# The length-49 stage of a second Fourier transform: from split products on 98 rows to plain float32 products in the four quarters of TensorE

## The chip, the cores and the metric

The kernel runs on one core of one Trainium2 chip. The metric is the device time of one execution in microseconds (us). The engines are TensorE (PE; its weight loads are listed as PEld), VectorE (DVE), ScalarE (ACT), GpSimd (POOL) and SyncE (SP), whose queue starts nearly all DMAs. A change of over 0.3% either way is counted here as faster or slower.

## The reference

Three blocks follow one another on x of shape (2, 3136, 256); the change touches the transform of the third.

```python
def reference(**kwargs):
    x = attn_out                       # rfft over 3136, 256x256 complex mix, soft threshold, irfft
    x = _moe_ref(x=x, **moe_kwargs)    # layer norm, 256 -> 1024 -> 256 with relu, residual
    return _moe2_ref(x=x, **moe2_kwargs)

def _moe2_ref(x, w_ch1, w_ch2):
    X = np.fft.fft(x, axis=1)
    X = np.fft.fft(X, axis=2)
    mixed = np.real(X).astype(np.float32)
    u = x + mixed
    mu = np.mean(u, axis=-1, keepdims=True)
    var = np.mean((u - mu) ** 2, axis=-1, keepdims=True)
    un = (u - mu) / np.sqrt(var + 1e-06)
    ch = np.maximum(un @ w_ch1, 0.0) @ w_ch2
    return (u + ch).astype(np.float32)
```

## The kernel before

**Numbers.** Most matmuls take an operand in the type float32r, cut to a high and a low part (`h`, `l`), and add three products (`mm3r`: high by high, low by high, high by low; lines 228, 229 and 230). The three lines serve the first layers of both multilayer perceptrons (into the PSUM tiles `psa`) and several transform stages (into `psc`). Other matmuls are plain float32 products: the first transform's input stage (L331), part of its inverse (L368, L556) and the length-64 stages (L499, L511, L852).

**Order of the work.** After the first block come 13 chunks of the first perceptron (`mlp1`, 512, 384 or 256 rows each), then 13 chunks of the second (`mlp2`). `run_mlp` records for each chunk eight steps `l1` (a `psa` tile each, cut into `h` and `l` by ACT at L765 and DVE at L767) and up to four steps `l2` (L784 and L785 into `psb`, added to the residual by DVE). Between them it calls hooks at places such as (8, "l1", 6), which means chunk 8 behind step 6 of `l1`. A scheduler lays out each engine's order from that, and each engine works through its own in order.

**The stage that is changed.** A length of 3136 is 49 times 64. `Stage98` does the length-49 part of the second transform for each of the two batches: it reads the output of `mlp1` from DRAM (`dX1`, 98 rows of 8192; row 2n+s holds n of 49 and s of 2), multiplies by a 98 by 98 matrix, and writes `dA2` in DRAM. The matrix never mixes the two values of s, so half of it is zeros. Each `step` takes 512 of the 8192 columns, 16 steps per batch:

- `load` brings the columns in (L396), `split` cuts them into `h` and `l`. For batch 0 POOL does both parts (L408, L218). For batch 1 POOL first folds channel c with channel 256-c (L416 to L418, into a tile `w`), then ACT makes `h` (L210) and POOL makes `l` (L218).
- `mm3r` adds three products on 98 partitions into one `psc` tile (three `psc` tiles exist).
- The result is copied to a tile `o`: for batch 0 with the folding on ACT (L467) and DVE (L471, L472), for batch 1 by ACT (L210). Channel 128 comes from a small product made once per batch (`middle2`, L222 to L224). SP stores `o` (L476).

Batch 0 is done beside chunks 8 to 10 of `mlp1` (hooks `STAGE4_AT`), batch 1 beside chunks 1 to 3 of `mlp2` (`STAGE4_MLP2`). `Front` reads `dA2` back later (L836) and does the length-64 stage (L852, `stage_b`) and the channel transform (L877, `dmix`) through `psc` and `w` tiles, of which there are four (`WB`).

## Time and profile before

| | |
|---|---|
| time, median of 3 runs | 788.33 us (786.74 to 789.31) |
| profiled execution, own time | 788.44 us |
| its span, first to last instruction | 786.6 us |
| PE busy | 778.3 us (99%) |
| PEld busy | 662.7 us (84%) |
| DVE busy | 557.8 us (71%) |
| ACT busy | 374.4 us (48%) |
| POOL busy | 180.9 us (23%) |
| DMA, mean | 121 GB/s |

The profiled execution lies within the three runs, and 1.8 us of its time lie outside its span. Matmuls are pipelined: one matmul's row in a list gives the time until its result is there, which is longer than the distance to the next. The distances are read from the chain of work that ended last, where each piece is as long as it held up the end.

### The profile page before, as it was taken

The numbers are of one execution on the slowest core, as the hardware profiler recorded it, in microseconds if no ns is written. First come the engines' busy times: TensorE is split into PE (matmuls) and PEld (weight loads), VectorE is DVE, ScalarE is ACT, GpSimd is POOL, SyncE is SP. The second block draws the span as 40 slices with busy tenths as digits, with TensorE's granted clock in tenths as the row PEclk, the third lists the DMA queues.
The fourth block names the chain that finished last, engine by engine and source line by source line (L and its number), as shares of the span: only waits on it lengthen the run. The fifth ranks groups of instructions, "written<-read, shape, count | busy, mean of one in ns | idle before, by whom it ended". The sixth has DMA issues, their size and how long they took to land.

```text
span 786.6 us, 12135 instructions
## 1 busy us (share of the span) xinstructions
PE 778.3 (99%) x4306; PEld 662.7 (84%) x4306; DVE 557.8 (71%) x1253; ACT 374.4 (48%) x807; POOL 180.9 (23%) x198
## 2 busy tenths in 40 slices
PE   8999999999999999999999999999999999999997
PEld 3889987978888888988888998888888898888886
DVE  6799977687855889867875778546646657666643
ACT  0544356447954444555532346456643535444421
POOL 0464321263511111144420002466300000000000
PEclk9999999999999999999999999999999999999999
DMA  8951200630257233355743336554543334422211
GB/s 215 264 164 53 62 20 1 217 111 28 81 181 261 76 106 121 126 155 169 233 146 118 105 99 164 167 150 134 157 118 101 102 119 122 109 71 76 61 33 41
DMA packets 78911, 95.16 MB, mean 121 GB/s; under 512 B 17538, under 2 KB 59274, under 8 KB 78656
## 3 DMA queue, kind: packets, MB, share of 16 engines
q1 hardware_dynamic: 78772, 94.33, 39.9%
q8 instruction: 34, 0.56, 0.3%
q14 instruction: 25, 0.20, 0.1%
q10 hardware_dynamic: 80, 0.07, 0.0%
HBM read 56.89 MB, written 37.49 MB: 120 GB/s over the span
## 4 chain that ended last, share of the span: by engine, by line
PE 89%; DVE 4%; DMA 3%; issue 1%; SPq 1%; ACT 0%; POOL 0%; POOLq 0%; DVEq 0%
PE psb L784 23%; PE psb L785 12%; PE psa L228 12%; PE psa L230 11%; PE psa L229 11%; PE psb L532 5%; PE psc L852 3%; PE psc L228 2%; PE psc L230 2%; PE psc L229 2%; PE psc L368 2%; PE psa L499 2%; PE psc L877 1%; DMA q<-in_x_dram 1%; PE psc L553 1%
## 5 line engine op out<-in xcount | busy, mean ns | idle before, releaser
L765 ACT ACTIVATE h<-psa 128x512 fp32r<-128x512 f32 (+2 forms) x208 | 117.3, 572 | 198.8 <-PE psa L230 145.3
L767 DVE SCALAR_TENSOR_TENSOR h<-psa,h 128x512 fp32r<-128x512 f32 (+2 forms) x208 | 135.1, 654 | 61.9 <-ACT h L765 58.5
L784 PE MATMUL psb<-r3a,h 128*128 128x512 f32 x392 | 137.2, 395 | 0.0
L784 PE MATMUL psb<-r2b,h 128*128 128x512 f32 x392 | 136.8, 397 | 0.1
L785 PE MATMUL psb<-r3a,h 128*128 128x256 f32 x392 | 106.5, 281 | 0.0
L785 PE MATMUL psb<-r2b,h 128*128 128x256 f32 x392 | 105.9, 281 | 0.0
L532 PE MATMUL psb<-wm,h 128*128 128x256 f32 (+1 forms) x600 | 90.4, 297 | 0.1
L784 PEld LDWEIGHTS psb<-r2b,h 128*128 128x128 f32 x392 | 71.7, 188 | 15.9 <-issue 0.8
L784 PEld LDWEIGHTS psb<-r3a,h 128*128 128x128 f32 x392 | 71.9, 188 | 15.2
L532 PEld LDWEIGHTS psb<-wm,h 128*128 128x128 f32 (+1 forms) x600 | 78.1, 188 | 7.6 <-issue 5.5
L228 PE MATMUL psa<-u0r,r2b 128*128 128x512 f32 (+2 forms) x208 | 80.6, 388 | 0.0
L228 PE MATMUL psa<-u0r,r3a 128*128 128x512 f32 (+1 forms) x208 | 79.5, 382 | 0.0
L229 PE MATMUL psa<-u0r,r3a 128*128 128x512 f32 (+1 forms) x208 | 78.6, 378 | 0.0
L229 PE MATMUL psa<-u0r,r2b 128*128 128x512 f32 (+2 forms) x208 | 78.5, 378 | 0.0
L230 PE MATMUL psa<-u0r,r2b 128*128 128x512 f32 (+2 forms) x208 | 78.1, 380 | 0.0
L785 PEld LDWEIGHTS psb<-r3a,h 128*128 128x128 f32 x392 | 73.9, 189 | 3.9
L785 PEld LDWEIGHTS psb<-r2b,h 128*128 128x128 f32 x392 | 74.0, 189 | 3.3
L230 PE MATMUL psa<-u0r,r3a 128*128 128x512 f32 (+1 forms) x208 | 76.2, 378 | 0.0
L790 DVE TENSOR_TENSOR o<-psb,yb 128x256 f32<-128x256 f32 x74 | 30.3, 419 | 57.2 <-PE psb L785 55.9
L210 ACT ACTIVATE yg<-psc 98x512 f32<-98x512 f32 (+2 forms) x58 | 49.6, 866 | 37.7 <-PE psc L553 20.5
L218 POOL TENSOR_TENSOR u0r<-w,u0r 98x512 fp32r<-98x512 f32 (+2 forms) x28 | 37.3, 1346 | 95.5 <-ACT u0r L210 95.5
L218 POOL TENSOR_TENSOR h<-w 128x512 f32<-128x512 f32 (+1 forms) x26 | 34.7, 1335 | 84.5 <-DVE w L539 77.9
(141 smaller groups left out, 1368.2 us busy)
## 6 DMA issues: line engine op xcount, KB each, us to landing
dT<-q SPq DMA_DIRECT2D x19, 512.0 KB
q<-dT SPq DMA_DIRECT2D x19, 512.0 KB
s<-in_moe_w_ch_dram SPq DMA_DIRECT2D x16, 512.0 KB
dA<-o SPq DMA_DIRECT2D x32, 196.0 KB
dY<-yg SPq DMA_DIRECT2D x12, 512.0 KB
r<-dA SPq DMA_DIRECT2D x48, 128.0 KB
dX<-o SPq DMA_DIRECT2D x10, 512.0 KB
yb<-dX SPq DMA_DIRECT2D x50, 64.0 KB
```

The source lines that it names most:

```text
L210: nc.scalar.activation(out=o, in_=i, func=AF.Copy, scale=scale)
L218: ins = eng.tensor_tensor(out=o, in0=a, in1=b, op=ALU.subtract)
L228: nc.tensor.matmul(out=ps, lhsT=lh, rhs=rh, start=first, stop=False)
L229: nc.tensor.matmul(out=ps, lhsT=ll, rhs=rh, start=False, stop=False)
L230: ins = nc.tensor.matmul(out=ps, lhsT=lh, rhs=rl, start=False, stop=last)
L532: nc.tensor.matmul(out=ps[0:m, u * D:(u + 1) * D], lhsT=xv[:, o:o + m], rhs=wm_hl[wv][:, e, c, :], start=k == 0, stop=k == 11)
L765: ins = nc.scalar.activation(out=h[:, 0:n], in_=ps[:, 0:n], func=AF.Relu)
L767: ins = nc.vector.scalar_tensor_tensor(out=l[:, 0:n], in0=ps[:, 0:n], scalar=0.0, in1=h[:, 0:n], op0=ALU.max, op1=ALU.subtract)
L784: nc.tensor.matmul(out=ps, lhsT=h[:, ts_], rhs=w2[:, f, :], start=f == 0, stop=False)
L785: ins = nc.tensor.matmul(out=ps[:, 0:D], lhsT=l[:, ts_], rhs=w2[:, f, 0:D], start=False, stop=f == NF - 1)
L790: nc.vector.tensor_tensor(out=o, in0=ps[:, 0:D], in1=self.y[:, i, :], op=ALU.add)
L852: nc.tensor.matmul(out=ps, lhsT=self.raw[p][0:n, k, q * 128:(q + 1) * 128], rhs=self.cols(n, pr[k][1], im), start=True, stop=True)
```

## The change

Each step now takes 1024 columns, in two groups e of 512, so there are 8 steps per batch. The rows of s=0 lie on partitions 0 to 48 and those of s=1 on partitions 64 to 112. `quad` issues four plain float32 products per step: the product of s and e takes its 49 rows from the half s of the partitions, a 49 by 64 table from the same half, and writes 64 partitions in the half e of the PSUM tile of s. A step so fills two `psc` tiles. Splitting is gone; the folding of batch 1 stays and its result is the matmul's operand. The products for channel 128 take the same form with 16 columns. `dA2` is written by 64 stores of 49 rows where there were 32 of 98. The hooks go from 16 to 8 per batch.

```diff
@@ -14,7 +14,7 @@
 YB, HB, WB, SB = 4, 9, 4, 2
-R98, S98, O98 = 4, 8, 4
+R98, O98 = 4, 4
...
-STAGE4_AT = ((8, "l1", 6), (8, "l1", 7)) + tuple((8, "l2", i) for i in range(4)) + tuple(
-    (9, *at) for at in (("l1", 1), ("l1", 3), ("l1", 5), ("l2", 0), ("l2", 1), ("l2", 3))) + tuple(
-    (10, *at) for at in (("l1", 1), ("l1", 3), ("l1", 5), ("l2", 0)))
-STAGE4_MLP2 = tuple(
-    (1, *at) for at in (("l1", 1), ("l1", 3), ("l1", 5), ("l2", 0), ("l2", 1), ("l2", 2), ("l2", 3))) + tuple(
-    (2, *at) for at in (("l1", 1), ("l1", 3), ("l1", 5), ("l2", 0), ("l2", 1), ("l2", 3))) + tuple(
-    (3, *at) for at in (("l1", 1), ("l1", 3), ("l1", 5)))
+STAGE4_AT = ((8, "l1", 7), (8, "l2", 1), (8, "l2", 3), (9, "l1", 1), (9, "l1", 6), (9, "l2", 2), (10, "l1", 3), (10, "l2", 0))
+STAGE4_MLP2 = ((1, "l1", 3), (1, "l2", 0), (1, "l2", 2), (2, "l1", 1), (2, "l1", 5), (2, "l2", 1), (3, "l1", 1), (3, "l1", 5))
 STAGE4_FROM = ((7, "l2", 0), (0, "l1", 5))
...
@@ -107,7 +95,10 @@
     cs = ca.copy()
     for q in range(0, 96, 4):
         cs[:, q:q + 2], cs[:, q + 2:q + 4] = -ca[:, q + 2:q + 4], ca[:, q:q + 2]
-    t["ca"] = np.concatenate([ca, cs], 1)
+    cq = np.zeros((128, 128))
+    for s in range(2):
+        cq[64 * s:64 * s + N1, 0:N1], cq[64 * s:64 * s + N1, 64:64 + N1] = ca[s::2, s::2], cs[s::2, s::2]
+    t["ca"] = cq
     t["cam"] = cam.reshape(NQ, 128)
     t["cim"] = cim.reshape(128, NQ)
...
@@ -250,14 +239,13 @@
 
 
     ident = cp.tile([128, 128], F32, name="ident")
-    ca_hl = cp.tile([NQ, 2, 2 * NQ], F32R, name="ca_hl")
+    ca = cp.tile([128, 128], F32, name="ca")
     cam = cp.tile([NQ, 128], F32, tag="cam", name="cam")
     cam_hl = cp.tile([NQ, 2, 128], F32R, tag="cd", name="cam_hl")
     cim_hl = cp.tile([128, 2, NQ], F32R, name="cim_hl")
     cb = cp.tile([128, NK + 1, 128], F32, name="cb")
     cb0 = cp.tile([N2, 102], F32, name="cb0")
     ci0 = cp.tile([68, N2], F32, name="ci0")
-    ca_h, ca_l, cs_h, cs_l = (ca_hl[:, i % 2, i // 2 * NQ:(i // 2 + 1) * NQ] for i in range(4))
     g_sb = cp.tile([128, 2], F32, name="g_sb")
     e4 = cp.tile([128, 1], F32, name="e4")
 
...
@@ -373,70 +361,62 @@
             v = yg[self.b].rearrange("p j c -> p (j c)")
             sp.dma_start(out=dY[self.b][16 * c:min(16 * c + 16, NQ), :], in_=v[c:96:6, :] if c < 6 else v[96:98, :])
 
-    def s98():
-        return [next(s98_ring)[0:NQ] for _ in range(2)]
-
-
     class Stage98:
 
 
 
-        def __init__(self, src, dst, ch, cl, tag):
-            self.src, self.dst, self.ch, self.cl, self.tag = src, dst, ch, cl, tag
-            self.raw, self.hl = {}, {}
+        def __init__(self, src, dst, tag):
+            self.src, self.dst = (a.rearrange("(n s) f -> s n f", s=2) for a in (src, dst))
+            self.tag, self.raw, self.out = tag, {}, {}
             self.fold_last = src is dX1[0]
             self.g = self.nl = self.ns = 0
 
         def load(self):
             g = self.nl
-            if g >= 16:
+            if g >= 8:
                 return
-            n = 1 if self.fold_last else 2
-            t = wk.tile([NQ, 512], F32, tag="t98", name="r98", bufs=TB) if self.fold_last else stg()[0:NQ]
-            sp.dma_start(out=t, in_=self.src[:, g * 512:(g + n) * 512])
-            for e in range(n):
-                self.raw[g + e] = t[:, e * 512:(e + 1) * 512]
-            self.nl += n
-
-        def split(self):
+            t = next(s98_ring)
+            for s in range(2):
+                sp.dma_start(out=t[64 * s:64 * s + N1], in_=self.src[s][:, g * 1024:(g + 1) * 1024])
+            self.raw[g] = [t[:, e * 512:(e + 1) * 512] for e in range(2)]
+            self.nl += 1
+
+        def fold(self):
             g = self.ns
-            if g >= 16:
+            if g >= 8 or self.fold_last:
                 return
-            t = self.raw.pop(g)
-            if self.fold_last:
-                h, l = s98()
-                nc.gpsimd.tensor_copy(h, t)
-                sub(nc.gpsimd, l, t, h)
-                self.hl[g] = (h, l)
-                self.ns += 1
-                return
-            f = wslot(n=NQ)
-            v, w = (a.rearrange("q (j c) -> q j c", c=D) for a in (t, f))
-            lo, hi = v[:, :, 1:128], v[:, :, 255:128:-1]
-            nc.gpsimd.tensor_tensor(out=w[:, :, 1:128], in0=lo, in1=hi, op=ALU.add)
-            nc.gpsimd.tensor_tensor(out=w[:, :, 129:256], in0=lo, in1=hi, op=ALU.subtract)
-            nc.gpsimd.tensor_copy(w[:, :, 0:256:128], v[:, :, 0:256:128])
-            h, l = s98()
-            a_copy(h, f)
-            sub(nc.gpsimd, l, f, h)
-            self.hl[g] = (h, l)
+            for e in range(2):
+                f = wslot()
+                v, w = (a.rearrange("q (j c) -> q j c", c=D) for a in (self.raw[g][e], f))
+                lo, hi = v[:, :, 1:128], v[:, :, 255:128:-1]
+                nc.gpsimd.tensor_tensor(out=w[:, :, 1:128], in0=lo, in1=hi, op=ALU.add)
+                nc.gpsimd.tensor_tensor(out=w[:, :, 129:256], in0=lo, in1=hi, op=ALU.subtract)
+                nc.gpsimd.tensor_copy(w[:, :, 0:256:128], v[:, :, 0:256:128])
+                self.raw[g][e] = f
             self.ns += 1
 
+        def quad(self, c, v, n=512):
+
+            ps = [psum(self.tag) for _ in range(2)]
+            for e in range(2):
+                for s in range(2):
+                    ins = nc.tensor.matmul(out=ps[s][64 * e:64 * e + 64, 0:n], lhsT=ca[64 * s:64 * s + N1, c:c + 64],
+                                           rhs=v[e][64 * s:64 * s + N1], start=True, stop=True)
+            mark["pe"] = getattr(ins, "ins", ins)
+            return ps
+
         def middle(self):
 
-            t = wk.tile([NQ, 32], F32, tag="m98", name="m98", bufs=1)
-            hl = wk.tile([NQ, 2, 32], F32R, tag="mhl", name="mhl", bufs=1)
-            sp.dma_start(out=t, in_=self.src.rearrange("q (j c) -> q j c", c=D)[:, :, 128])
-            self.mid_in = t, hl
+            t = wk.tile([128, 32], F32, tag="m98", name="m98", bufs=1)
+            for s in range(2):
+                sp.dma_start(out=t[64 * s:64 * s + N1], in_=self.src[s].rearrange("n (j c) -> n j c", c=D)[:, :, 128])
+            self.mid_in = t.rearrange("q (g e j) -> q e g j", e=2, j=2)
 
         def middle2(self):
-            t, hl = self.mid_in
-            nc.gpsimd.tensor_copy(hl[:, 0], t)
-            sub(nc.gpsimd, hl[:, 1], t, hl[:, 0])
-            ps = psum(self.tag)
-            mm3(ps[0:NQ, 0:32], cs_h, cs_l, hl[:, 0], hl[:, 1], True, True)
-            self.mid = wk.tile([NQ, 32], F32, tag="mid", name="mid", bufs=1)
-            a_copy(self.mid, ps[0:NQ, 0:32])
+            ps = self.quad(64, [self.mid_in[:, e] for e in range(2)], 16)
+            self.mid = wk.tile([128, 2, 16], F32, tag="mid", name="mid", bufs=1)
+            for s in range(2):
+                a_copy(self.mid[:, s], ps[s][:, 0:16])
 
         def start(self):
             self.middle()
@@ -444,36 +424,35 @@
             self.load()
 
         def ahead(self):
-            self.split()
-            if self.fold_last:
-                self.load()
-            self.split()
+            self.load()
+            self.fold()
 
         def step(self):
             g = self.g
-            if g >= 16:
+            if g >= 8:
                 return
             if g == 0:
                 self.middle2()
-            if self.nl <= g + (3 if self.fold_last else 4):
+            if self.nl <= g + 3:
                 self.load()
-            self.split()
-            h, l = self.hl.pop(g)
-            ps = psum(self.tag)
-            mm3r(ps[0:NQ, :], self.ch, self.cl, h, l, True, True)
-            o = wk.tile([NQ, 512], F32, tag="r98", name="o98", bufs=R98) if self.fold_last and g % 2 else next(o98_ring)[0:NQ]
-            if self.fold_last:
-                v, w = (a.rearrange("q (j c) -> q j c", c=D) for a in (ps[0:NQ, :], o))
-                ins = nc.scalar.activation(out=w[:, :, 0:128], in_=v[:, :, 0:128], func=AF.Copy)
-                with tc.issue_after(getattr(ins, "ins", ins)):
-                    a_copy(w[:, :, 128], self.mid[:, 2 * g:2 * g + 2])
-                lo, hi = w[:, :, 1:128], v[:, :, 255:128:-1]
-                nc.vector.tensor_tensor(out=w[:, :, 129:256], in0=lo, in1=hi, op=ALU.subtract)
-                nc.vector.tensor_tensor(out=lo, in0=lo, in1=hi, op=ALU.add)
-            else:
-                a_copy(o, ps[0:NQ, :])
-                nc.gpsimd.tensor_copy(o[:, 128:512:256], self.mid[:, 2 * g:2 * g + 2])
-            sp.dma_start(out=self.dst[:, g * 512:(g + 1) * 512], in_=o)
+            self.fold()
+            ps = self.quad(0, self.raw.pop(g))
+            for s in range(2):
+                o = wk.tile([128, 512], F32, tag="r98", name="o98", bufs=R98) if self.fold_last and s else next(o98_ring)
+                mid = self.mid[:, s, 2 * g:2 * g + 2]
+                if self.fold_last:
+                    v, w = (a.rearrange("q (j c) -> q j c", c=D) for a in (ps[s], o))
+                    ins = nc.scalar.activation(out=w[:, :, 0:128], in_=v[:, :, 0:128], func=AF.Copy)
+                    with tc.issue_after(getattr(ins, "ins", ins)):
+                        a_copy(w[:, :, 128], mid)
+                    lo, hi = w[:, :, 1:128], v[:, :, 255:128:-1]
+                    nc.vector.tensor_tensor(out=w[:, :, 129:256], in0=lo, in1=hi, op=ALU.subtract)
+                    nc.vector.tensor_tensor(out=lo, in0=lo, in1=hi, op=ALU.add)
+                else:
+                    a_copy(o, ps[s])
+                    nc.gpsimd.tensor_copy(o[:, 128:512:256], mid)
+                for e in range(2):
+                    sp.dma_start(out=self.dst[s][:, (2 * g + e) * 512:(2 * g + e + 1) * 512], in_=o[64 * e:64 * e + N1])
             self.g += 1
 
 
@@ -966,9 +945,7 @@
     todo = {}
 
     def l_ca():
-        t = stg()[0:NQ, 0:4 * NQ]
-        sp.dma_start(out=t, in_=t_ca.rearrange("q h c -> q (h c)"))
-        a_copy(flat(ca_hl), t)
+        sp.dma_start(out=ca, in_=t_ca)
         halves(cim_hl, tab["cim"])
 
     def l_cim():
...
@@ -1155,9 +1132,9 @@
 
     for ch in mlp1[1:12] + mlp2[1:]:
         ch.by_act = True
-    s98_ring = ring(u0[:, 0:4096], S98, 512)
+    s98_ring = ring(u0[:, 0:4096].bitcast(F32), 4, 1024)
     o98_ring = ring(cp.tile([128, O98 * 512], F32, tag="wm", name="o98"), O98, 512)
-    s4 = [Stage98(dX1[b], dA2[b], ca_h, ca_l, "c") for b in range(NB)]
+    s4 = [Stage98(dX1[b], dA2[b], "c") for b in range(NB)]
     hooks = {}
 
     def after(k, i, f):
```

PE, behind a step of the second layer in chunk 8 of `mlp1`; before (`ca_hl` is the split table, `psc` the stage's PSUM tile):

```order
L784 MATMUL psb<-r3a,h 128x512
L785 MATMUL psb<-r3a,h 128x256
L228 MATMUL psc<-u0r,ca_hl 98x512
L229 MATMUL psc<-u0r,ca_hl 98x512
L230 MATMUL psc<-u0r,ca_hl 98x512
L228 MATMUL psa<-u0r,r3a 128x512
```

The same place now (line numbers are those of the changed file, in which L228 to L230 are L217 to L219 and L784 and L785 are L763 and L764; `x4` stands for four rows in a line):

```order
L763 MATMUL psb<-r3a,h 128x512
L764 MATMUL psb<-r3a,h 128x256
L403 MATMUL psc<-u0r,ca 64x512 x4
L217 MATMUL psa<-u0r,r3a 128x512
L218 MATMUL psa<-u0r,r3a 128x512
```

Four float32 products stand together where three float32r products stood, for twice the columns. 14 of the 16 steps stand so. The other two, both of batch 0, stand in two pieces; PE in chunk 9, before:

```order
L785 MATMUL psb<-r3a,h 128x256
L228 MATMUL psc<-u0r,ca_hl 98x512
L229 MATMUL psc<-u0r,ca_hl 98x512
L230 MATMUL psc<-u0r,ca_hl 98x512
L228 MATMUL psc<-u0r,ca_hl 98x512
L229 MATMUL psc<-u0r,ca_hl 98x512
L230 MATMUL psc<-u0r,ca_hl 98x512
L230 MATMUL psa<-u0r,r3a 128x512
```

And now:

```order
L219 MATMUL psa<-u0r,r3a 128x512
L403 MATMUL psc<-u0r,ca 64x512 x2
L217 MATMUL psa<-u0r,r3a 128x512
L218 MATMUL psa<-u0r,r3a 128x512
L219 MATMUL psa<-u0r,r3a 128x512
L217 MATMUL psa<-u0r,r3a 128x512
L218 MATMUL psa<-u0r,r3a 128x512
L219 MATMUL psa<-u0r,r3a 128x512
L403 MATMUL psc<-u0r,ca 64x512 x2
L217 MATMUL psa<-u0r,r3a 128x512
```

The two products of group 0 and the two of group 1 are apart, with six products of the first layer between them. With the products for channel 128, PE goes to quarters and back 19 times: 10 times in batch 0 and 9 times in batch 1.

## Rows read from the trace of the kernel before

**Rows 1.** The page, part 1 (busy us, share, instructions) and part 2 (slices).

```profile
PE 778.3 (99%) x4306; PEld 662.7 (84%) x4306; DVE 557.8 (71%) x1253; ACT 374.4 (48%) x807; POOL 180.9 (23%) x198
...
PE   8999999999999999999999999999999999999997
```

**Rows 2.** The page, part 4: the chain that ended last, by engine.

```profile
PE 89%; DVE 4%; DMA 3%; issue 1%; SPq 1%; ACT 0%; POOL 0%; POOLq 0%; DVEq 0%
```

**Rows 3.** Windows: a plain chunk, batch 0's stretch, batch 1's stretch.

```profile
core 0: us, PE busy (x) PEld busy (x) DVE busy (x) ACT busy (x) POOL busy (x), PEclk, DMA share, GB/s
...
258.20:280.40 22.20, 22.20 (x114) 18.81 (x113) 20.24 (x45) 10.56 (x23) 3.28 (x2) 1.00 0.36 120
354.50:420.00 65.50, 65.50 (x325) 53.93 (x324) 48.16 (x116) 31.70 (x85) 23.22 (x24) 1.00 0.54 170
490.00:569.00 79.00, 78.86 (x418) 65.68 (x417) 45.99 (x117) 44.41 (x98) 44.82 (x74) 1.00 0.52 153
```

**Rows 4.** The stage's split table `ca_hl`: durations in ns (min/median/max), forms.

```profile
L228 PE MATMUL psc<-u0r,ca_hl x32: 391/394/479, 354.9 to 566.4; 98*98 98x512 f32 x32
L229 PE MATMUL psc<-u0r,ca_hl x32: 389/396/398, 355.2 to 566.7; 98*98 98x512 f32 x32
L230 PE MATMUL psc<-u0r,ca_hl x32: 389/397/472, 355.5 to 566.9; 98*98 98x512 f32 x32
```

**Rows 5.** Chain, 354.0 to 358.5 us: start, us held, what.

```profile
354.91 0.02 PE psc L222
354.93 0.09 PE psc L223
355.01 0.09 PE psc L224
...
357.25 0.23 PE psc L228
357.48 0.23 PE psc L229
357.71 0.23 PE psc L230
```

**Rows 6.** Chain, 103.0 to 104.8 us: a float32 product of 512 columns.

```profile
103.24 0.86 PE psc L368 x2
```

**Rows 7.** Timeline of PEld, 4.9 to 9.5 us: start, us, count, idle before.

```profile
5.39 0.19 PEld L331 LDWEIGHTS psa<-h,cam 98*128 98x128 f32 x1 [0.24 <-issue]
5.82 0.19 PEld L331 LDWEIGHTS psa<-h,cam 98*128 98x128 f32 x1 [0.24 <-issue]
6.25 0.19 PEld L331 LDWEIGHTS psa<-h,cam 98*128 98x128 f32 x1 [0.24 <-issue]
```

**Rows 8.** Line 556: float32 with 64 columns of weights.

```profile
L556 PE MATMUL psc<-h,ci x4: 379/404/430, 97.9 to 167.2; 68*64 68x256 f32 x4
```

**Rows 9.** Chain, 595.5 to 597.5 us: products on 64 rows, then 128.

```profile
596.27 0.58 PE psc L852 x4
596.85 0.42 PE psc L877 x2
```

**Rows 10.** Chain, 428.5 to 435 us: the same lines, all on 128 rows.

```profile
432.69 0.45 PE psc L877 x4
433.14 0.84 PE psc L852 x8
```

**Rows 11.** Line 218, 480 to 570 us: batch 1's low parts on POOL.

```profile
L218 POOL TENSOR_TENSOR u0r<-w,u0r x16: 1282/1293/1303, 489.6 to 558.6; 98x512 fp32r<-98x512 f32 x16
```

**Rows 12.** Line 408: batch 0's high parts on POOL.

```profile
L408 POOL CAST u0r<-r x16: 612/614/1080, 341.9 to 402.0; 98x512 fp32r<-98x512 f32 x16
```

**Rows 13.** Line 210, 480 to 570 us: batch 1's high parts and copies on ACT.

```profile
L210 ACT ACTIVATE u0r<-w x16: 613/629/638, 488.9 to 557.9; 98x512 fp32r<-98x512 f32 x16
L210 ACT ACTIVATE o<-psc x16: 577/597/609, 497.9 to 567.4; 98x512 f32<-98x512 f32 x16
```

**Rows 14.** Line 476: the stores of the stage on SP's queue.

```profile
L476 SPq DMA_DIRECT2D dA<-o x32: 307/322/2547, 357.4 to 568.3; - x32
```

**Rows 15.** Line 416: the first of batch 1's two folding operations.

```profile
L416 POOL TENSOR_TENSOR w<-stg x16: 725/732/912, 485.6 to 555.9; 98x254 f32<-98x254 f32 x16
```

More of the change, by code (lines that the diff above doesn't have):

```diff
@@ L69 @@
 NF = DFF // 128
-def _round12(v):
-    b = v.astype(np.float32).view(np.uint32).astype(np.uint64)
-    b += 0x7FF + (b >> 12 & 1)
-    return (b & 0xFFFFF000).astype(np.uint32).view(np.float32)
 def _tables():
@@ L161, in _tables @@
     out = {"ident": ident.astype(np.float32)}
-    for k in ("cam", "cim", "cb", "ci", "cb0", "ci0", "cd"):
+    for k in ("ca", "cam", "cim", "cb", "ci", "cb0", "ci0", "cd"):
         out[k] = t.pop(k).astype(np.float32)
-    for k, v in t.items():
-        h = _round12(v)
-        out[k] = np.ascontiguousarray(np.stack([h, _round12(v - h)], 1))
+    assert not t
     return out
```

## The prediction

> **What bounds the kernel now.** I read the page's busy times first: PE is busy 99% of the span and every slice between the first and the last is at 90% or more [rows 1]. The chain that ended last says the same: 89% of it is PE [rows 2]. Then the two stretches that the change touches, by windows. Beside batch 0 PE is busy all of 65.5 us, beside batch 1 78.86 of 79.0 us, at granted clock 1.00, while POOL, ACT and DVE have room: POOL 23.2 and 44.8 us, ACT 31.7 and 44.4 us [rows 3]. So a microsecond of PE's order in these stretches is a microsecond of the end, and work taken from POOL or ACT is worth nothing by itself. The reader should carry one number into the sum: how long PE is held, per 1024 columns, by the old and by the new form.
>
> **What is removed from PE.** The stage has 32 groups of three products [rows 4]. Their rows give 0.39 us each, but that is the time to the result; in the chain each holds PE 0.23 us [rows 5], in some places 0.24, so a group holds it 0.70 us and 1024 columns hold it 1.40 us. The three small products for channel 128 hold it 0.20 us (0.02, 0.09 and 0.09) [rows 5]. Removed: 32 x 0.70 + 2 x 0.20 = 22.8 us.
>
> **What one float32 product costs.** A plain float32 product of 512 columns stands in the trace as two matmuls, and both together hold the chain for 0.86 us [rows 6], 0.43 us each. Rows and weight columns do not enter: L331, on 98 rows with 128 columns of weights, goes at the same distance of 0.43 us [rows 7]. So the four products of a step are eight halves of 0.43 us, 3.44 us if nothing runs side by side and 0.86 us if all four quarters do. The old form took 1.40 us. Everything depends on where between these two it falls.
>
> **How the halves overlap.** No two matmuls of the old kernel use different parts of the array at once, so this must be bounded. What the trace does show is the order. In a row of float32 products the weights of each half are loaded 0.43 us after those of the half ahead (5.39, 5.82, 6.25 us) [rows 7], the distance of the matmuls themselves: here loads run one matmul ahead and not two. The halves of a product follow each other in the program and use the same quarter. So the second half of the first product must wait 0.43 us for its own quarter, and the first half of the second product stands behind it. It can then run beside that second half, from which it differs in rows, but not beside the first. I take this staircase as the likeliest: a product starts when the second half of the product ahead has started and its own weights are in. Those take 0.05 us for 64 columns: the float32 matmul with 64 weight columns lasts 430 ns where it waited for its load and 379 where it did not [rows 8]. Four products then take 3 x (0.43 + 0.05) + 0.86 = 2.30 us, two of them 0.48 + 0.86 = 1.34 us.
>
> **What going to quarters and back costs.** Line 852 has a few products on 64 rows, which are the nearest rows. Four of its matmuls behind full-size ones hold the chain 0.58 us, and the two of L877 behind them 0.42 [rows 9]; on 128 rows eight of L852 hold it 0.84, so four 0.42, and four of L877 0.45, so two 0.22 [rows 10]. Going there costs 0.16 us and coming back 0.20, together 0.36 us. For the low bound I keep nothing, in case quarters of 64 columns do not need it; I take 0.36, since these rows change the rows used as the new form does. The Trainium skill's page TensorEngine Tiling (Array Packing), section Key Properties, says that changing the tiling mode drains TensorE; the rows just named agree, with 0.36 us a round trip, and by the page's other statement, that a change of tile alone does not drain, there is nothing to add within a burst.
>
> **The sum on PE.** 14 steps stand as one burst: 14 x (2.30 + 0.36) = 37.2 us. Two steps stand in two pieces: 4 x (1.34 + 0.36) = 6.8 us. The products for channel 128 are eight short halves per batch, 0.05 us each by the weight load or 0.09 us by the old small products [rows 5]: 0.4 to 0.7 us, I take 0.5, together 1.0 us. One pair of them stands alone, one more round trip: 0.36 us. Added: 45.4 us. Less 22.8 us this is +22.6 us. The profiled execution took 788.44 us, 0.1 above the median, so the forecast is 811 us.
>
> **What else moves, and why it is set at nothing.** POOL loses 16 low parts of 1.29 us in batch 1 [rows 11] and 16 high parts of 0.61 us with their low parts in batch 0 [rows 12]; ACT loses 16 high parts of 0.63 us [rows 13]. None of it stands in the chain beside a PE that is always busy. The copies out of PSUM stay at two per 1024 columns and at 512 columns each; 0.60 us on ACT [rows 13]. SP gets 32 more stores, 8 more loads in batch 1 and two more small ones, 42 x 0.32 us [rows 14] = 13.4 us in some 130 us; the transposed inputs of later chunks go through the same queue and could land about 1 us later each. PE has no wait for them in these stretches today [rows 3], and a slower PE asks later. If that cover fell short in each of five chunks it would be about 5 us. Folding for batch 1 now writes into `w` tiles that are held until the burst. Two of the four are so taken, and `dmix` has to wait in three places until a burst has read its tile; DVE, which works in order, then holds back the next `l` part (L767). PE has three `psa` tiles of six products, 3 x 6 x 0.23 = 4.1 us, as cover against a burst of 2.66 us. Folding itself takes 2 x 2 x 0.73 us and two short copies per step [rows 15], where a step comes every 79/8 = 9.9 us, so PE should not wait for it. I take nothing, and up to 5 us for the range. With no cost for switching and no 0.05 us the likeliest case falls to 802 us; its own range is 802 to 816.
>
> **Rivals.**
> 1. *All four quarters at once.* If the second half of a product does not hold up the next product, a burst is 0.86 + 3 x 0.05 = 1.01 us and a piece 0.91. With switching: 14 x 1.37 + 4 x 1.27 + 1.36 = 25.6 us, +2.8 us, 791 us. Against it speaks the one-ahead order of the loads [rows 7]; for it, that nothing in the trace shows a matmul held up by another quarter. The Trainium skill, page TensorE: Matmul & The Clock Gate, section Part 3: Packing small matmuls, says that matmuls in different tiles start about 4 ns apart and run together; by that figure a burst is 0.87 us before switching, an estimate that gives about 789 us. The same section says that matmuls start and end in program order, which makes the staircase for products of two halves. No run shows yet which of the two holds here.
> 2. *All four at once, and no cost for switching*: 14 x 1.01 + 4 x 0.91 + 1.0 = 18.8 us, -4.0 us, 784 us. This is the case on the other side. It decides once a burst with all that surrounds it holds PE less than some 1.2 us. Against it stand the 0.58 and 0.42 us around line 852 [rows 9].
> 3. *Two streams*, one for each half of the rows, each in its own order: three halves one behind the other, 1.29 + 0.05 = 1.34 us. 14 x 1.70 + 4 x 1.27 + 1.36 = 30.2 us, +7.4 us, 796 us.
> 4. *No overlap at all*, the change does not do what it says: 3.44 us a burst and 1.72 a piece, 14 x 3.80 + 4 x 2.08 + 1.36 = 62.9 us, +40 us, 828 us. For it speaks that no row shows an overlap of matmuls at all.
>
> **Chances.** Staircase 0.47, no overlap 0.12, two streams 0.11, all at once with switching 0.12, all at once without 0.18. The range leaves out the case at 828 us and reaches to the others: 783 to 816 us. Faster by over 0.3% is the last case, 0.18. Within 0.3% is half of the fourth, 0.06. Slower is the rest, 0.76.
>
> **What the profile of the changed kernel would show.** For the staircase: in a burst of L403 the weight loads of the eight halves start about 0.05 and 0.43 us apart in turn, and the burst holds PE about 2.3 us. If all start within 0.2 us it is rival 1 or 2; if each is 0.43 us behind the last it is rival 4. For switching: 0.16 us of pause ahead of the first load of L403 and 0.20 behind the last. PE should still be busy near 99%; POOL should fall by some 50 us and ACT by some 10 us, with no gain in time. Idle on PE inside chunks 1 to 3 of `mlp2`, released by POOL's folding or by DVE, would mean that the `w` tiles are the new wait. I would be wrong above all if quarters are served out of the program's order, or if plain float32 in a quarter costs other than 0.43 us a half.

## The result and the profile after

| | before | after |
|---|---|---|
| time, median of 5 runs each on one chip | 788.33 us (786.74 to 789.46) | 794.15 us (793.66 to 797.29) |
| ratio, 95% interval | | 1.0086 (1.0059 to 1.0113) |
| profiled execution: own time, span | 788.44, 786.6 us | 795.9, 794.1 us |

The change made the kernel slower, by 5.8 us where 22.6 were forecast. The page of the changed kernel, parts 1, 2 and 4, answers to [rows 1, 2]:

```profile
PE 782.5 (99%) x4348; PEld 652.9 (82%) x4348; DVE 550.6 (69%) x1253; ACT 365.0 (46%) x792; POOL 127.5 (16%) x146
...
PE   9999999999999999999999999998999999999997
...
PE 80%; DMA 9%; DVE 6%; issue 2%; SPq 1%; ACT 1%; POOL 1%; POOLq 0%; DVEq 0%; ACTq 0%
```

POOL lost 53 us and ACT 9 us, as foreseen, and nothing came of it. The chain is where the reader should stop: PE's share of it fell from 89% to 80%, and DMA's rose from 3% to 9%. Transfers now end last in places where PE did. Busy shares do not show this: PE is still at 99%.

**The burst.** A burst is the four products of one step in a row. The timeline of PE, a window of 0.2 us from 363.90, and the same burst in a longer window (start, us, count):

```profile
363.97 0.66 PE L403 MATMUL psc<-u0r,ca 49*64 49x512 f32 x4
363.97 1.09 PE L403 MATMUL psc<-u0r,ca 49*64 49x512 f32 x8
```

Two windows on line 403 inside the burst (us, PE busy with the number of matmuls, PEld the same, granted clock, DMA share, GB/s):

```profile
364.05:364.44 0.39, 0.39 (x4) 0.12 (x8) 1.00 0.18 63
364.44:364.48 0.04, 0.04 (x8) 0.00 (x0) 1.00 0.25 102
```

The timeline of PEld from 363.9 to 364.0 us, and the group of these loads by line 403 (ns min/median/max, first and last start in us):

```profile
363.96 0.15 PEld L403 LDWEIGHTS psc<-u0r,ca 49*64 49x64 f32 x4 [0.25 <-issue]
```

```profile
L403 PEld LDWEIGHTS psc<-u0r,ca x64: 129/132/135, 355.9 to 416.9; 49*64 49x64 f32 x64
L403 PE MATMUL psc<-u0r,ca x64: 589/604/640, 356.0 to 417.3; 49*64 49x512 f32 x64
```

One half lasts up to 0.640 us until its result is there, and four of them together last 0.66 us. Four loads take 0.15 us where one takes 0.13, so they start some 7 ns apart. These are the first halves of all four products. Until 364.44 us nothing else runs; the four second halves follow together from 364.45 us, 0.48 us behind the first. All four quarters run side by side from the start, and there is no staircase.

What a burst costs is read from the chain, for a piece of two products (four halves) and for a whole burst:

```profile
361.31 1.01 PE psc L403 x4
362.31 0.32 PE psb L764
...
363.92 0.12 PE psb L764
364.04 1.02 PE psc L403 x8
365.06 0.43 PE psa L217
365.48 0.23 PE psa L218
```

A burst holds PE 1.02 us, and the matmul behind it 0.43 in place of 0.23: 1.22 us, where the old form held it 1.40. A piece of two is as dear, 1.01 + (0.32 - 0.12) = 1.21 us, for half the columns. The products for channel 128 add 0.1 us to the piece that they stand in (1.13 us in the chain at 355.89). In batch 1 one pair of them stands alone, at 502.04 us. The chain runs over transfers there, so the price is read from a kernel of the experiments (stores on POOL's queue, loads held back), where the same pair stands at 499.86 us:

```profile
499.93 0.22 PE psc L403 x4
500.15 0.43 PE psa L217
```

Alone it holds PE 0.22 + (0.43 - 0.23) = 0.42 us, and the other pair adds 0.1 us to its burst. So PE's own order is 14 x 1.22 + 4 x 1.21 + 0.1 + 0.5 = 22.5 us against the 22.8 removed. By that the kernel should have come out even (-0.3 us).

**The waits.** PE's waits between 420 and 610 us in the changed kernel (what waited for whom, us in all, times, longest); before, PE was busy 78.86 of 79.0 us in batch 1's stretch [rows 3]:

```profile
PE psb L763 <- DVE mv L644: 1.8, 1, 1.8
PE psa L217 <- ACT u0r L199: 1.5, 1, 1.5
PE psa L217 <- DVE h L746: 0.5, 1, 0.5
PE psc L831 <- DMA r<-dA: 0.4, 1, 0.4
```

The timeline of PE at the first of them, and two windows behind the two long ones (us, PE busy, PEld, DVE, ACT, POOL, granted clock, DMA share, GB/s):

```profile
521.34 0.47 PE L763 MATMUL psb<-r2b,h 128*128 128x512 f32 x1 [1.77 <-DVE mv L644]
...
522.11 0.40 PE L763 MATMUL psb<-r2b,h 128*128 128x512 f32 x1
...
522.48 0.63 PE L763 MATMUL psb<-r2b,h 128*128 128x512 f32 x1
```

```profile
522.50:525.80 3.30, 3.30 (x12) 2.48 (x10) 1.54 (x5) 3.30 (x9) 2.26 (x7) 0.50 0.27 64
553.20:556.50 3.30, 3.30 (x8) 2.59 (x9) 2.13 (x9) 3.30 (x9) 0.00 (x0) 0.50 0.20 65
```

Behind each long wait stands a stretch at the lower clock level, 1.2 GHz (0.50), in which the same matmul takes 0.63 us and not 0.40. Each such stretch of at least 3.3 us does half its work, some 1.7 us lost. The waits at 519.57, 537.64 and 550.85 us and the two stretches make 1.77 + 0.51 + 1.48 + 2 x 1.7 = 7.2 us. With the 0.4 us for `r<-dA` and PE's order that is 7.3 us; the two profiled executions lie 7.5 us apart.

What is late at the two long waits is the transposed input of the next chunk (`dT<-q`, then `q<-dT` through SP; ACT and DVE cut it into parts, L199 and L207). SP's queue, ACT and DVE in the changed kernel, and behind them SP's two rows in the kernel before:

```profile
480.65 2.55 SPq L412 DMA_DIRECT2D m<-dX  x1
483.25 9.62 SPq L380 DMA_DIRECT2D u0r<-dX  x10
492.96 1.09 SPq L635 DMA_DIRECT2D yb<-dX  x2
494.15 1.85 SPq L779 DMA_DIRECT2D out_dram<-o  x3
496.05 0.54 SPq L635 DMA_DIRECT2D yb<-dX  x1
496.80 1.84 SPq L690 DMA_DIRECT2D dT<-q  x1
...
506.49 0.75 SPq L698 DMA_DIRECT2D q<-dT  x1
```

```profile
515.79 1.15 ACT L199 ACTIVATE u0r<-q 128x512 fp32r<-128x512 f32 x2 [5.82 <-DMA q<-dT]
516.46 1.29 DVE L207 TENSOR_TENSOR u0r<-q,u0r 128x512 fp32r<-128x512 f32 x2 [5.76 <-ACT u0r L199]
```

```profile
493.07 0.57 SPq L711 DMA_DIRECT2D dT<-q  x1
503.63 0.38 SPq L719 DMA_DIRECT2D q<-dT  x1
```

The ninth and tenth load of the stage (the fifth group) have no free place until POOL has folded the first group, so SP waits, and `dT<-q` behind them goes out 3.7 us later than before. DVE is done with its part at 517.75 us and only then comes to what stands behind it in its order, the additions that empty `psb` among it (L769 and L770, from 520.06 us); for these PE waits at 519.57 us. The short wait at 537.64 us has another origin: ACT could not copy into `o` until a store of the stage, `dA<-o` of 527.99 us, had landed at 536.18 us, and the cut of a `psa` tile that PE needed free stood behind that copy, on ACT and then on DVE.

### The profile page after: what moved, and what is told of

It is laid out like the page before. It is cut to its first block, busy times and chain, and to the rows that moved or that the text cites. A ratio compares the mean times of both kernels' runs of the same rounds, so it can differ in the third digit from the quotient of the medians.

```text
span 794.1 us, 12190 instructions
## 1 busy us (share of the span) xinstructions
PE 782.5 (99%) x4348; PEld 652.9 (82%) x4348; DVE 550.6 (69%) x1253; ACT 365.0 (46%) x792; POOL 127.5 (16%) x146
## 4 chain that ended last, share of the span: by engine, by line
PE 80%; DMA 9%; DVE 6%; issue 2%; SPq 1%; ACT 1%; POOL 1%; POOLq 0%; DVEq 0%; ACTq 0%
PE psb L763 21%; PE psa L217 11%; PE psb L764 11%; PE psa L219 10%; PE psa L218 10%; PE psb L511 5%; PE psc L831 2%; DMA q<-dT 2%; DMA dA<-o 2%; PE psc L356 2%; PE psa L478 2%; PE psc L403 2%; DMA q<-in_x_dram 1%; PE psc L856 1%; PE psc L532 1%
## 5 line engine op out<-in xcount | busy, mean ns | idle before, releaser
L763 PE MATMUL psb<-r2b,h 128*128 128x512 f32 x392 | 138.5, 400 | 1.8 <-DVE mv L644 1.8
L763 PE MATMUL psb<-r3a,h 128*128 128x512 f32 x392 | 137.3, 396 | 0.0
L764 PE MATMUL psb<-r2b,h 128*128 128x256 f32 x392 | 106.9, 282 | 0.0
L764 PE MATMUL psb<-r3a,h 128*128 128x256 f32 x392 | 106.1, 281 | 0.0
L763 PEld LDWEIGHTS psb<-r2b,h 128*128 128x128 f32 x392 | 72.5, 189 | 19.0 <-issue 3.8
L763 PEld LDWEIGHTS psb<-r3a,h 128*128 128x128 f32 x392 | 71.8, 188 | 16.3 <-ACT h L744 0.8
L217 PE MATMUL psa<-u0r,r2b 128*128 128x512 f32 (+2 forms) x208 | 82.4, 396 | 2.0 <-ACT u0r L199 1.5
L217 PE MATMUL psa<-u0r,r3a 128*128 128x512 f32 (+1 forms) x208 | 80.0, 384 | 0.1
L219 PE MATMUL psa<-u0r,r2b 128*128 128x512 f32 (+2 forms) x208 | 79.5, 386 | 0.0
L218 PE MATMUL psa<-u0r,r2b 128*128 128x512 f32 (+2 forms) x208 | 79.2, 381 | 0.0
L764 PEld LDWEIGHTS psb<-r3a,h 128*128 128x128 f32 x392 | 73.9, 189 | 5.5 <-issue 1.6
L764 PEld LDWEIGHTS psb<-r2b,h 128*128 128x128 f32 x392 | 74.7, 190 | 2.9
L219 PE MATMUL psa<-u0r,r3a 128*128 128x512 f32 (+1 forms) x208 | 76.2, 378 | 0.0
L769 DVE TENSOR_TENSOR o<-psb,yb 128x256 f32<-128x256 f32 x74 | 30.3, 419 | 63.0 <-PE psb L764 62.6
L199 ACT ACTIVATE yg<-psc 98x512 f32<-98x512 f32 (+2 forms) x58 | 49.6, 867 | 37.9 <-PE psc L532 20.8
L217 PEld LDWEIGHTS psa<-u0r,r2b 128*128 128x128 f32 x208 | 39.6, 190 | 13.2 <-ACT u0r L199 2.8
L207 POOL TENSOR_TENSOR h<-w 128x512 f32<-128x512 f32 (+1 forms) x26 | 34.7, 1334 | 84.7 <-DVE w L518 78.1
```

The source lines that it names most:

```text
L199: nc.scalar.activation(out=o, in_=i, func=AF.Copy, scale=scale)
L207: ins = eng.tensor_tensor(out=o, in0=a, in1=b, op=ALU.subtract)
L217: nc.tensor.matmul(out=ps, lhsT=lh, rhs=rh, start=first, stop=False)
L218: nc.tensor.matmul(out=ps, lhsT=ll, rhs=rh, start=False, stop=False)
L219: ins = nc.tensor.matmul(out=ps, lhsT=lh, rhs=rl, start=False, stop=last)
L763: nc.tensor.matmul(out=ps, lhsT=h[:, ts_], rhs=w2[:, f, :], start=f == 0, stop=False)
```

## The experiments

The edits are to the changed kernel. Ratios are to the kernel before on the same chip, with 95% intervals. The first theory was called "SP" (the order on SP's queue makes the transposed inputs late). Its rivals are "w tiles" (the folded groups hold tiles that others need), "PE order" (the bursts themselves cost the time), "no slack" (a wait that is moved away comes back elsewhere) and "transfers" (the stage's traffic delays the inputs, whatever queue starts it).

### Loads and w tiles

The first run puts the later loads of batch 1 behind the trip of the transposed input. The second gives the folded groups tiles of their own. The third does both.

```diff
             if self.nl <= g + 3:
-                self.load()
+                with ExitStack() as es:
+                    if not self.fold_last:
+                        es.enter_context(tc.issue_after(self.gate.trip))
+                    self.load()
```

```diff
-                f = wslot()
+                if e == 0:
+                    both = stg()
+                f = both[:, e * 512:(e + 1) * 512]
```

> Batch 1's loads from the fourth group of 1024 columns on stand on SP's queue behind the transposed input's trip of the chunk after next; the orders of PE, ACT, DVE and POOL stay as they are. Theory 'SP': the fifth group's load stood on SP until POOL had folded the first group (492.3 us), and dT<-q behind it went out at 496.8 us. It should now go out near 492.5, q<-dT should land some 4 us earlier than 515.8, and PE's wait of 1.77 us at 519.6 should go with the window of half clock behind it (1.7 us): 794.2 - 3.5 = 790.7 us; if the waits at 537.6 and 550.9 us go too, 787 us. Theory 'w tiles' (the folded groups take tiles that dmix and ACT's work need) and theory 'PE order' (the loss is in the bursts themselves): 794 us, no change.

> Folded groups of batch 1 go into two tiles of 1024 columns that nothing else uses there, and take none of the four w tiles. Theory 'w tiles': POOL folds the second group at once instead of at 503.7 us, dmix and the l parts behind it do not wait, and most of the 5.8 us comes back: 789 us. Theory 'SP': the fifth group's load still waits on SP for the first fold, dT<-q still goes out after 496 us and PE still waits near 519 us: 793 to 794 us. Theory 'PE order': 794 us.

> Both edits at once: loads of batch 1 behind the trips on SP, folded groups in tiles of their own. Theories 'SP' and 'w tiles' together: no wait of PE over 0.3 us is left between 490 and 575 us, the clock stays at its upper level there, and what is left is PE's own order, 1.1 us in batch 0 less 8 x 0.18 us in batch 1: 788 us, within 0.3% of the kernel before. If it stays at 793 us or more, the loss is neither.

Measured: 792.91 us, 1.0041 (1.0028 to 1.0055); 799.66 us, 1.0130 (1.0111 to 1.0149); 794.06 us, 1.0054 (1.0038 to 1.0069). In the first, `dT<-q` went out at 493.34 us and the wait at 519 us was gone with its stretch of low clock. But new waits stood later, the longest of 2.45 us at 600.8 us for the transposed input of another chunk. "SP" was right on the place and too small. "w tiles" fell: with tiles of its own POOL folded earlier, two more loads went out on SP directly behind `dT<-q`, and PE waited 7.1 us for the transposed inputs in three places. Both edits together were no better than the first alone, and stayed above the 793 us from which the expectation had called the loss neither; the next runs show what "SP" had left out.

### Which batch

Batch 0 alone and batch 1 alone in the new form; the other keeps the old class, table and hooks.

> Batch 0 in the new form, batch 1 in the old form of split products. If the loss sits in batch 1's stretch (theories 'SP' and 'w tiles'), this kernel has only batch 0's part: six whole bursts at -0.18 us, four pieces at +0.5 us, the products for channel 128: +1.1 us, 789.4 us, and PE busy without a gap between 490 and 575 us. If the bursts themselves cost the time (theory 'PE order'), about half of 5.8 us: 791 us or more.

> Batch 0 new, batch 1 old, as in the run of that kind before, whose own table load held ACT and so PE for 3.54 us at 440 us with 6.8 us of half clock behind it; the table's copy now stands 20 and more instructions later on ACT. Without that wait 797.1 - 3.5 - 3.4 = 790.2 us is left; by theory 'SP', batch 0 costs 1.1 us, 1.0014 of the kernel before. If the bursts cost the time, 792 us or more.

> Batch 0 old, batch 1 new, with the loads where the changed kernel has them. Theory 'SP': the late dT<-q and q<-dT are in this half alone, so PE waits near 519 and 551 us with half clock behind, as in the changed kernel: 5.8 - 1.1 = +4.7 us, 793 us. Theory 'PE order' with batch 1's eight whole bursts: 8 x 1.22 us in place of 8 x 1.40 us, 787 us, and no waits.

Measured: 797.12 us, 1.0093 (1.0079 to 1.0106); 791.20 us, 1.0015 (1.0000 to 1.0029); 798.62 us, 1.0106 (1.0089 to 1.0124). The first says nothing of batch 0, since ACT waited 8.27 us for the table that only this kernel loads there; the second is the same kernel without that wait. Batch 0 costs 1.2 us by the second (0 to 2.3 by its interval); its bursts and pieces cost by the rows above 6 x 1.22 + 4 x 1.21 + 0.1 - 8 x 1.40 - 0.2 = +0.9 us. The rest lies in batch 1, though its bursts are cheaper than what they replace, so "PE order" fell too. The third lost more than the whole change and nearly twice what was expected of it. It has a wait of 1.80 us from 517.9 us again, and one of 2.49 us at 605 us for the transposed input of a later chunk, which the changed kernel does not have. So the two parts do not add up to the whole; why that input is late only there stays open.

### Steps earlier

Late loads as in the first run, the last steps of batch 1 one to three hooks earlier; in the second run those of batch 0 too.

```diff
-STAGE4_MLP2 = (... (2, "l1", 5), (2, "l2", 1), (3, "l1", 1), (3, "l1", 5))
+STAGE4_MLP2 = (... (2, "l1", 5), (2, "l2", 0), (2, "l2", 2), (3, "l1", 2))
-STAGE4_AT = (... (9, "l1", 6), (9, "l2", 2), (10, "l1", 3), (10, "l2", 0))
+STAGE4_AT = (... (9, "l1", 5), (9, "l2", 0), (9, "l2", 3), (10, "l1", 4))
```

> The first edit (loads of batch 1 behind the trips on SP) and, besides, batch 1's last two steps three to four hooks earlier, the last behind step 2 of chunk 3's first layer instead of step 5. Theory 'read-back': with the loads out of the way PE's wait of 2.45 us at 600.8 us came from r<-dA, which stands on SP until the stage's last stores have landed (issued 577.3 us, in the kernel before 572.9), with dT<-q and q<-dT behind it. It should now go out some 3 us earlier, and the wait and its window of half clock (1.7 us) should go: 792.9 - 4.2 = 788.7 us, within 0.3% of the kernel before. Rival 'no slack': the transposed inputs are late in one chunk or another whatever is moved, a wait of 1 to 3 us shows up elsewhere, and it stays at 792 to 794 us.

> As the run above, and batch 0's last three steps one to two hooks earlier too. Theory 'read-back': PE's short wait at 429.6 us for r<-dA of batch 0 (0.27 to 0.44 us) and the 0.8 us that the kernel falls back there go: 788 us. Rival 'no slack': as above, 792 us or more, with the waits in other chunks.

Measured: 793.50 us, 1.0050 (1.0038 to 1.0063); 792.81 us, 1.0040 (1.0028 to 1.0052). "Read-back" held for batch 0, whose wait at 429 us went in the second run. For batch 1 it fell: all but 0.35 us of the wait at 600 us went, and others came, 1.43 us at 546 in the one and 1.19 at 545 in the other. SP shows why (second run):

```profile
520.08 3.60 SPq L458 DMA_DIRECT2D dA<-o  x4
523.77 0.44 SPq L693 DMA_DIRECT2D dT<-q  x1
...
533.30 2.78 SPq L380 DMA_DIRECT2D u0r<-dX  x2
536.13 0.72 SPq L701 DMA_DIRECT2D q<-dT  x1
```

The four stores of a step hold SP for 3.60 us ahead of `dT<-q`, the two loads of a group for 2.78 us ahead of `q<-dT`. It goes out at 536.13 us, in the kernel before at 532.97, although PE stood 1.0 us ahead of the kernel before at the start of this stretch. So the wait had only moved, as "no slack" has it, and the stores looked like the second half of the theory "SP".

### Another queue

All loads and stores of batch 1's steps go on POOL's queue; in the second run batch 0's last steps are early too.

```diff
-                sp.dma_start(out=t[64 * s:64 * s + N1], ...
+                (sp if self.fold_last else nc.gpsimd).dma_start(out=t[64 * s:64 * s + N1], ...
-                    sp.dma_start(out=self.dst[s][:, ...
+                    (sp if self.fold_last else nc.gpsimd).dma_start(out=self.dst[s][:, ...
```

> All of batch 1's loads and stores of the stage are issued on POOL's queue instead of SP's; POOL folds and copies the middle channels itself, so it waits there for what it has to wait for anyway. Theory 'SP order' (steps of twice the size put two loads and four stores at a time on SP, each waiting for POOL or ACT, and the transposed inputs behind them): dT<-q and q<-dT of chunks 1 to 4 of the second perceptron go out as in the kernel before, ACT and DVE get them in time, PE has no wait over 0.5 us between 490 and 610 us, and 794 falls to 789 us, 1.000 to 1.002 of the kernel before. Rival 'transfers': the stage's traffic itself delays the transposed inputs, whatever queue issues it; PE's waits stay and the time stays at 793 us or more.

> As the run above, and batch 0's last three steps one to two hooks earlier, which took the wait for r<-dA at 429.6 us away in an earlier run (PE then stood 0.2 us ahead of the kernel before ahead of batch 1). Theory 'SP order': eight bursts of batch 1 at -0.18 us each come on top: 787.5 us, 0.997 to 0.999 of the kernel before. Rival 'transfers': 792 us or more.

Measured: 790.95 us, 1.0020 (1.0002 to 1.0038); 789.32 us, 0.9997 (0.9983 to 1.0011). The loss is gone but for 0.2%, then wholly, so what SP had to issue was most of it. The gain expected on top in the second run cannot be told from none. Single executions of the first lie between 789.5 and 795.7 us, and the profiled one, the longest, still has waits of 2.3 and 1.8 us near 517 and 522: in it eight loads left POOL within 4.3 us, and the two `yb` behind `m` on SP took 6.06 us to issue, so that `dT<-q` went out at 498.25 us. In the profiled execution of the second run the same eight loads left as fast, but the `yb` took 3.39 us and `dT<-q` went out at 493.21. That "transfers" has a part in the long executions is so argued, not shown.

Then the two kinds apart, all with batch 0's last steps early: only the stores on POOL's queue; only the loads; the stores there and the loads late on SP as in the first run.

> Only the stores of batch 1 on POOL's queue, its loads on SP as in the changed kernel (ten ahead of dT<-q, four ahead of the next), batch 0's last steps early. If the loads hold up the transposed inputs: dT<-q is out after 495 us again, PE waits 1 to 2 us near 519 us and again in the next chunk, with half clock behind one of them: 791 to 793 us, 1.002 to 1.005 of the kernel before. If only the stores did: 789.3 us as with both on POOL's queue.

> Only the loads of batch 1 on POOL's queue, its stores on SP, batch 0's last steps early. If the stores hold up the transposed inputs too: no wait near 519 us over 1 us, but waits between 530 and 610 us as in the run with late loads and early steps: 791 to 793 us. If only the loads did: 789.3 us.

> Stores on POOL's queue, loads on SP but behind the trips of the transposed input, batch 0's last steps early. By theory 'SP order' this is as good as all of it on POOL's queue, 789.3 us, 0.999 to 1.001 of the kernel before. If it stays above 1.003, what POOL's queue took away was not the order on SP.

Measured: 793.05 us, 1.0037 (1.0023 to 1.0050); 793.89 us, 1.0055 (1.0034 to 1.0076); 787.08 us, 0.9960 (0.9948 to 0.9972). With either kind left on SP as it was, 0.4 to 0.6% of loss stays. The second run missed its expectation: with the loads on POOL's queue, and no store of the stage on SP ahead of that transposed input, PE still waited 1.39 us from 515.5 and 1.78 us from 520.0 us: the `yb` took 6.16 us to issue and `dT<-q` went out at 497.26 us, again in the longest execution. So the transposed input can be late with the early loads on POOL's queue too. Holding them back behind it, as in the third run, did better than moving them (0.9960 against 0.9997, intervals apart), and better than the theory "SP order" had said. With both kinds out of the way the new form beats the kernel before, on the same four products per step. SP, ACT, the windows of [rows 3] and the chain by engine of this last kernel:

```profile
481.56 3.72 SPq L380 DMA_DIRECT2D u0r<-dX  x6
...
490.98 1.81 SPq L693 DMA_DIRECT2D dT<-q  x1
...
501.30 0.76 SPq L701 DMA_DIRECT2D q<-dT  x1
502.11 3.42 SPq L380 DMA_DIRECT2D u0r<-dX  x1
```

```profile
509.66 1.16 ACT L199 ACTIVATE u0r<-q 128x512 fp32r<-128x512 f32 x2 [1.86 <-DMA q<-dT]
```

```profile
354.00:420.00 66.00, 66.00 (x345) 47.12 (x344) 44.15 (x114) 31.01 (x86) 0.00 (x0) 1.00 0.51 166
490.00:569.00 79.00, 79.00 (x452) 61.81 (x452) 46.02 (x120) 36.92 (x84) 42.49 (x92) 1.00 0.50 155
```

```profile
PE 92%; DVE 4%; issue 1%; DMA 1%; SPq 1%; ACT 0%; POOL 0%; POOLq 0%; DVEq 0%
```

PE is busy without a gap, and its share of the chain is above that of the kernel before. The transposed input leaves 5.8 us earlier than in the changed kernel, and ACT waits 1.86 us for it and not 5.82.

### The staircase by itself

The products are halved in columns and put into two orders, everything else unchanged.

```diff
-            for e in range(2):
-                for s in range(2):
+            for e, s, k in ((e, s, k) for e in range(2) for s in range(2) for k in range(m)):
```

> Each product of 512 columns is made as two of 256, and the two of one quarter stand next to each other in the program (quarter 1, 1, 2, 2, 3, 3, 4, 4): as much work, in eight products of two halves of 0.21 us. The staircase of the prediction, in the form that a product whose quarter is busy holds up all behind it: the third product starts 0.43 us after the first, the fifth 0.87, the seventh 1.3 us, and a burst lasts 3 x 0.43 + 0.86 = 2.2 us. Theory 'each quarter has its own order': all four quarters start within 0.05 us, a burst lasts 1.0 to 1.1 us as in the changed kernel.

> The same eight products of 256 columns per burst, in the order quarter 1, 2, 3, 4, 1, 2, 3, 4. Both theories: four start together, and the burst lasts 1.0 to 1.1 us. The run is the measure for the one with neighbours: if that one lasts 2.2 us and this one 1.0 us, the order in the program decides; if both last 1.0 to 1.1 us, a busy quarter does not hold up the others.

Measured, one run each: 795.95 and 794.29 us. The timeline of PE in the run with neighbours, a short and a longer window:

```profile
364.55 0.47 PE L405 MATMUL psc<-u0r,ca 49*64 49x256 f32 x4
364.55 1.11 PE L405 MATMUL psc<-u0r,ca 49*64 49x256 f32 x16
```

and in the run in turn:

```profile
364.71 1.09 PE L405 MATMUL psc<-u0r,ca 49*64 49x256 f32 x16
```

Sixteen halves last 1.1 us in either order, not 2.2. With neighbours, too, four start within 0.04 us (0.47 us together, the longest single one 0.43), although the second product in the program belongs to a quarter that is busy. The first four loads, with neighbours and in turn:

```profile
364.55 0.17 PEld L405 LDWEIGHTS psc<-u0r,ca 49*64 49x64 f32 x4 [0.25 <-ACT q L673]
364.70 0.15 PEld L405 LDWEIGHTS psc<-u0r,ca 49*64 49x64 f32 x4 [0.25 <-ACT q L673]
```

One load lasts 0.13 us, so they start 13 ns apart with neighbours and 7 ns apart in turn: twice as far where twice as many products stand between them, so the program's order was indeed the one asked for. A busy quarter does not hold up what stands behind it for another.

### Whole bursts

Everything of batch 1 on POOL's queue, batch 0's steps early, and each step's products in one section that the scheduler may not divide.

```diff
+            with tc.tile_critical():
```

> All of batch 1's transfers on POOL's queue, batch 0's last steps early, and the four products of every step kept together, so that no step stands in two pieces. By the traces a piece of two holds PE 1.2 us where half a step of the old form took 0.70, a whole burst 1.22 where a step took 1.40: two steps whole save 2 x (2.4 - 1.22) = 2.4 us: 787 us, 0.997 of the kernel before. Keeping them together also moves other work on PE, and where that makes PE wait, the gain is gone: 789 us or more.

Measured: 853.19 us, 1.0784 (1.0762 to 1.0806). The bursts are whole, but the section waits for all that its four products need before the first may start: PE stands some 40 us in waits, up to 8.5 us each, for read-backs, stores and copies, and its mean granted clock is 0.966. Where little is waited for, the section still costs: at 426.98 us PE stands idle for 0.43 us ahead of the burst, released by nothing that the profile shows. What whole bursts alone would give stays open; that a piece costs as much as a burst is read from the chain only.

## Why the prediction was wrong, point by point

- **What bounds the kernel**: this was right. POOL and ACT were relieved for nothing.
- **What is removed, and 0.43 us a half**: this was right. Inside a burst the second halves come 0.48 us behind the first, which is 0.43 and the 0.05 us that the prediction took for the weights.
- **How the halves overlap**: this step failed. It took the order of the loads in [rows 7], where each product uses the same quarter as the one ahead, and let "the first half of the second product" stand behind the second half of the first. The two orders of 256 columns show that it does not. A whole burst holds PE 1.22 us and not 2.66, a piece 1.21 and not 1.70: 14 x 1.44 + 4 x 0.49 = 22.1 us too much. The Trainium skill, page TensorE: Matmul & The Clock Gate, section Part 3: Packing small matmuls, says both that matmuls of different tiles run together and that they start and end in program order. The records agree with the first and, for products of two halves, not with the second; the measurement decides.
- **Going to quarters and back**: this was right. A round trip costs 1.22 - 0.86 = 0.36 us, of which 0.20 behind the burst, as worked out from [rows 9, 10]. The Trainium skill's page TensorEngine Tiling (Array Packing), section Key Properties, names the drain; the trace agrees, with these 0.36 us.
- **Channel 128**: it was taken as 0.5 us a batch and one round trip for the pair that stands alone, 1.36 us. The pair does stand alone, in batch 1, but holds PE only 0.42 us with its trip, and all the rest 0.2 us: 0.7 us too much.
- **What else moves, set at nothing**: this step failed too, by the 6.1 us between PE's order (-0.3) and the result (+5.8). The cover named for SP was that PE had no wait there and that a slower PE asks later. PE was not slower. And what counted was not 42 x 0.32 us of issue but what the issues wait for: twice as many columns a step put two loads and four stores at a time on SP, each waiting for POOL or ACT, with `dT<-q` and `q<-dT` behind them. The bound of "about 5 us" was of the right size but a little short, and it had no term for the two stretches of lower clock, some 3.4 us.
- **The w tiles**: the wait of DVE behind `dmix` was not what cost. Tiles of their own made it worse, and with the loads held back as well they gained nothing.
- **The rivals**: PE did what the first one said, all four at once with switching, at 1.22 us a burst and not 1.37. By that alone it would have been even with the kernel before (-0.3 us); the waits on the transposed inputs made it slower. With them out, 787.08 us against 790.43.
- **What was luck**: the kernel came out slower, as forecast, and within the stated range, but not for the forecast reason. A cost of some 22.8 us that is not there and one of 6.1 us that was set at nothing partly cancel, and the first rival's 791 us comes close by the same kind of accident.

The gain of 3.4 us in the version with the stores on POOL's queue and the loads held back is more than PE's order explains. By it batch 0 costs 0.9 us and batch 1 saves 8 x 0.18 - 0.3 = 1.1 us. In the profiled executions 1.28 us of the lead arise ahead of the stage: at the same matmul of the second layers PE is 1.28 us ahead of the kernel before at 339.5 us, where the other versions in the new form, the whole bursts apart, lie between 1.2 us ahead and 0.4 behind; 0.48 us ahead at 481.4 us, behind batch 0; and 2.90 us ahead at 578.3 us, behind batch 1. So batch 0 costs 0.8 us, as the rows have it, and batch 1 saves 2.4 us. Where the rest of that comes from stays open. The kernel before was not run with its own loads and stores moved in this way, so how much of the gain belongs to the new form is not shown.

## What to carry to other kernels

Before a stage is made coarser, look at what each of its transfers waits for and what stands behind it in the same queue: the same bytes in larger lumps can hold up a transfer that PE needs, at no change in PE's busy share. Here it helped more to hold the early loads back behind the urgent transfer than to start them from another queue. When the share of DMA in the chain grows while PE stays at 99%, look for stretches of lower clock behind short waits; here they doubled the price of a wait. An order seen among products that share a part of the array says nothing about products that do not.

## What the runs showed of the hardware

- Float32 products in four quarters start some 7 ns apart, the first halves of a burst ahead of any second half, which follow 0.48 us later. A busy quarter does not block the next product in the program: with neighbours in one quarter the other quarters start 13 ns apart.
- A trip to quarters and back costs 0.36 us whether two or four products run in it (1.21 and 1.22 us).
- A PE wait of 1.5 to 1.8 us was followed by 3.3 us or more at 1.2 GHz in two places of the changed kernel, which cost as much again.
